# K^T V of a linear attention by 64x64 quadrants of TensorE, one head per quadrant

## The chip, the cores and the metric

The kernel runs on one core of a Trainium2 chip. The metric is the time of one execution in microseconds of the device. A profile is taken of one execution; its span, from the first to the last instruction, is about 2 us shorter than the time. The effect in this case is only about half a per cent, so traces are compared stage by stage, and the times come from several rounds (a round runs the compared kernels one after the other). TensorE's matmul side is PE in the profile and its weight loads are PEld; DVE is VectorE, ACT ScalarE, POOL GpSimd, SP the engine that issues most DMAs.

## The reference, cut to what matters

```python
# q, k, v: 8 batches, 8 heads, 576 positions, 64 values, float32
q_s = softmax(q, over the 64 values)
k_s = softmax(k, over the 576 positions)
kv  = einsum('bhsd,bhse->bhde', k_s, v)        # 64 x 64 per head: "K^T V"
x   = einsum('bhsd,bhde->bhse', q_s, kv)       # "X"; reordered to 4608 x 512
out = (silu(x @ w_gate) * (x @ w_val)) @ w_out # 512 -> 1536 -> 512
```

Nearly all arithmetic is in the last line. K^T V is small, but it runs on the same TensorE.

## The kernel before

A batch is handled in two groups G of four heads. A group's four heads are two row halves (g: partitions 0 to 63 and 64 to 127) times two column halves (h); `ek` holds exp(k), `vb` the values in bfloat16. Nine slices t of 64 positions are summed up in PSUM. A matmul takes the weights `lhsT` (here exp(k) of two heads, 64 rows x 128 columns) and streams `rhs` (the values of the same two heads and a column of ones, 129 values) past them. So it makes a 128 x 129 product, of which two 64 x 64 blocks are wanted and the last column is the softmax's sum:

```python
vbs = [const.tile([128, T, 130], BF16, ...) for i in range(2)]      # column 128 is ones

def kv_mm(b, G, kv, c):
    for t in range(T):                        # T = 9
        for g in range(2):
            r = slice(64 * g, 64 * g + 64)
            nc.tensor.matmul(
                out=kv[g][:, c:c + 129], lhsT=ek_of(b, G, g, t), rhs=vbs[G][r, t, 0:129],
                start=(t == 0), stop=(t == T - 1),
            )

def scale_both(b):                            # divide by the sum, on DVE
    ...
    nc.vector.reciprocal(out=kvr, in_=kv[:, :, 128])
    nc.vector.tensor_mul(kn[:, g], kv[:, :, 0:128], kvr.to_broadcast([128, NG, 128]))
```

X uses the wanted blocks as weights and the transposed q (`qt`) as stream; it already runs in 64x64 quadrants. In batches 2 to 7 `qt` comes from a transposing DMA, in batches 0 and 1 from TensorE. The order of TensorE's work:

```python
# batch 1 (after the first gate/value chunk), one group at a time
kv_one(1, 0); scale_one(1, 0, ...); norm_mul(1, 1)   # norm_mul: DVE makes qs
p = o_mm(2); x_one(1, 0); o_out(2, p)
turn_pe(1, 1, 0); turn_pe(1, 1, 1); ...              # transposes of qs on TensorE
kv_one(1, 1); scale_one(1, 1, ...)
p = o_mm(3); ... x_one(1, 1); o_out(3, p)

# batches 2 to 7: both groups together, within a chunk of 12 matmul units
for m in range(MT):
    ...                                              # exp, norm, turn_dma(b, G): qt by DMA
    if att and m == 8:
        kv_both(b); scale_both(b)
        if b + 1 < B: load_batch(b + 1)
    m_unit(c0, n, m)                                 # 8 matmuls of 448 or 512 values
    if att and m == 9:
        x_both(b)
```

The softmax here doesn't subtract the row's maximum and nothing guards it: scores larger than these inputs give would overflow.

## Time and profile before

| | before |
|---|---|
| time, median | 317.4 us |
| span in the profile | 316.2 us |
| PE busy | 306.3 us, 97% |
| granted TensorE clock | full (mean 1.000) |
| K^T V in the chain that ended last | about 3% |

From the page of the kernel before: its heading, the busy time of each engine (us, share of the span, instructions), and the start of the chain that ended last, that is of the work followed back from the last instruction.

```profile
span 316.2 us, 4851 instructions
PE 306.3 (97%) x1865; PEld 152.5 (48%) x1894; DVE 163.3 (52%) x277; ACT 147.1 (47%) x216; POOL 28.1 (9%) x35
PE 88%; DMA 4%; DVE 3%; ACT 2%; issue 1%; POOL 1%; SPq 0%; DVEq 0%
```

The third line is not a list of busy engines but of who was being waited for. That PE has 88% of it says more than its 97% busy time: the kernel ends when TensorE's stream of instructions ends.

The timeline of the kernel before around K^T V of batches 2 and 3 (start us, length us, engine, line, operation, output<-inputs, shape, count; in brackets the idle time before and what ended it):

```profile
66.13 1.22 PE L191 MATMUL kv<-vb,ek 64*128 64x129 bf16 x36
67.28 0.93 PE L298 MATMUL g_ps<-xt,wg 128*128 128x448 bf16 x4
70.42 0.69 PE L267 MATMUL xp<-qt,kn 64*64 64x512 bf16 x16
98.34 1.22 PE L191 MATMUL kv<-vb,ek 64*128 64x129 bf16 x36
99.50 0.82 PE L298 MATMUL g_ps<-xt,wg 128*128 128x512 bf16 x3
```

(A few records are missing: "x3" where there are four.)

### The profile page before, as it was taken

Reading aid. Unit: us, or ns where it says so; the run is one execution under the profiler, and the core shown is the slowest. Engines: PE = TensorE matmul, PEld = TensorE weight load, DVE = VectorE, ACT = ScalarE, POOL = GpSimd, SP = SyncE. Lnnn points to the kernel's source line nnn. Section 1 sums busy time; section 2 is a strip of 40 time slices with the busy share of each in tenths; the row PEclk is TensorE's granted clock in tenths of the full one; section 3 lists DMA queues with packets and bytes.
Section 4 is the critical chain, followed back from the end, with each engine's and each line's share of the span. In section 5 each row is a group of like instructions: output and inputs, shape, how many; then the busy total and the mean of one; then the engine's idle time right before and its main releaser. Section 6 shows DMA issues by size and latency. Waiting matters only on the chain.

```text
span 316.2 us, 4851 instructions
## 1 busy us (share of the span) xinstructions
PE 306.3 (97%) x1865; PEld 152.5 (48%) x1894; DVE 163.3 (52%) x277; ACT 147.1 (47%) x216; POOL 28.1 (9%) x35
## 2 busy tenths in 40 slices
PE   6999999999999999999999999999999999999994
PEld 2577744554444444544454444544444444444443
DVE  3734476685763567455835492639354333423421
ACT  4753397634663465447354637355743113312300
POOL 2930021101100020002000200020000000000000
PEclk9999999999999999999999999999999999999999
DMA  7999999269246906490629353944310202020124
GB/s 279 170 203 207 291 395 392 73 152 370 49 94 162 350 18 131 112 387 18 141 67 313 136 109 67 317 167 103 66 40 0 66 2 66 0 68 4 30 68 102
DMA packets 39304, 45.75 MB, mean 145 GB/s; under 512 B 16368, under 2 KB 23024, under 8 KB 39280
## 3 DMA queue, kind: packets, MB, share of 16 engines
q1 hardware_dynamic: 32480, 39.99, 42.0%
q0 software_dynamic: 6640, 5.31, 10.9%
q8 instruction: 15, 0.25, 0.3%
q10 hardware_dynamic: 160, 0.13, 0.2%
q14 instruction: 9, 0.07, 0.1%
HBM read 37.75 MB, written 9.44 MB: 149 GB/s over the span
## 4 chain that ended last, share of the span: by engine, by line
PE 88%; DMA 4%; DVE 3%; ACT 2%; issue 1%; POOL 1%; SPq 0%; DVEq 0%
PE g_ps L298 29%; PE u_ps L298 29%; PE o_ps L322 25%; PE kv L191 3%; DMA wv<-in_moe_w_val_dram 2%; DMA k<-in_k_dram 2%; DVE rs L138 1%; PE xp L267 1%; DVE qs L152 1%; PE o_ps L342 1%; ACT L124 1%; ACT eq L124 1%; POOL v L360 0%; PE tp L166 0%; POOL v L357 0%
## 5 line engine op out<-in xcount | busy, mean ns | idle before, releaser
L305 ACT ACTIVATE sg<-g_ps 128x512 bf16<-128x512 f32 (+2 forms) x120 | 65.2, 554 | 138.9 <-PE g_ps L298 119.4
L306 DVE TENSOR_TENSOR hr<-sg,u_ps 128x512 bf16<-128x512 bf16 (+2 forms) x120 | 74.5, 629 | 87.7 <-PE u_ps L298 80.3
L298 PE MATMUL g_ps<-xt,wg 128*128 128x512 bf16 (+2 forms) x469 | 110.0, 357 | 1.0 <-ACT xt L111 0.2
L298 PE MATMUL u_ps<-xt,wv 128*128 128x512 bf16 (+2 forms) x468 | 109.7, 357 | 1.0 <-DMA wv<-in_moe_w_val_dram 0.4
L322 PE MATMUL o_ps<-wo,hr 128*128 128x512 bf16 x414 | 93.0, 379 | 0.4 <-issue 0.2
L298 PEld LDWEIGHTS <-wv 128*128 128x128 bf16 x480 | 46.8, 98 | 47.2 <-DMA wv<-in_moe_w_val_dram 0.9
L298 PEld LDWEIGHTS <-wg 128*128 128x128 bf16 x480 | 45.8, 98 | 45.3 <-issue 0.9
L322 PEld LDWEIGHTS <-hr 128*128 128x128 bf16 x420 | 41.0, 98 | 49.1
L113 DVE COPY o_sb<-o_ps 128x512 f32<-128x512 f32 x33 | 22.4, 680 | 39.2 <-PE o_ps L322 37.3
L127 POOL CAST vb<-v 128x1152 bf16<-128x1152 f32 x14 | 16.1, 1148 | 173.5 <-DMA v<-in_v_dram 138.0
L138 DVE TENSOR_REDUCE rs<-eq 128x18 f32<-128x1152 bf16 (+2 forms) x18 | 21.7, 1214 | 12.8 <-ACT eq L124 12.8
L152 DVE TENSOR_TENSOR qs<-eq,rr 128x1152 bf16<-128x1152 bf16 (+2 forms) x18 | 22.0, 1232 | 0.1
L124 ACT ACTIVATE eq<-q 128x1152 bf16<-128x1152 f32 (+2 forms) x18 | 18.2, 1053 | 3.4 <-DMA q<-in_q_dram 3.4
L124 ACT ACTIVATE ek<-k 128x1152 bf16<-128x1152 f32 x16 | 18.0, 1159 | 0.7 <-DMA k<-in_k_dram 0.6
L305 ACT ACT_TABLE_LOAD x12 | 15.4, 1283 | 0.2
L124 ACT ACT_TABLE_LOAD x11 | 14.1, 1283 | 0.2
L387 PE MATMUL idle<-zero 128*128 128x512 bf16 x20 | 7.8, 555 | 2.7 <-DVE rs L138 1.5
L191 PE MATMUL kv<-vb,ek 64*128 64x129 bf16 x252 | 8.7, 217 | 0.0
L191 PEld LDWEIGHTS <-ek 64*128 64x128 bf16 x252 | 7.3, 94 | 2.7 <-ACT sg L305 2.1
L275 ACT CAST xt<-xp 128x512 bf16<-128x512 f32 x12 | 6.4, 589 | 3.6 <-PE xp L267 3.6
L276 DVE CAST xt<-xp 128x512 bf16<-128x512 f32 x12 | 7.7, 681 | 0.0
L113 DVE CAST xt<-xp 128x128 bf16<-128x128 f32 (+2 forms) x14 | 4.9, 374 | 2.8 <-PE xp L220 2.8
(45 smaller groups left out, 66.3 us busy)
## 6 DMA issues: line engine op xcount, KB each, us to landing
q<-in_q_dram SPq DMA_DIRECT2D x16, 576.0 KB, 5.3
k<-in_k_dram SPq DMA_DIRECT2D x16, 576.0 KB, 7.3
out_dram<-o_sb SPq DMA_DIRECT2D x70, 128.0 KB, 2.3
v<-in_v_dram SPq DMA_DIRECT2D x14, 576.0 KB, 9.0
wo<-in_moe_w_out_dram POOLq DMA_DIRECT2D x4, 384.0 KB, 16.4
wg<-in_moe_w_gate_dram POOLq DMA_DIRECT2D x2, 384.0 KB, 9.8
wv<-in_moe_w_val_dram POOLq DMA_DIRECT2D x2, 384.0 KB, 10.8
wg<-in_moe_w_gate_dram POOLq DMA_DIRECT2D x1, 512.0 KB, 13.8
```

The costliest lines, as they stand in the source:

```text
L113: eng.tensor_copy(out=out, in_=in_)
L124: nc.scalar.activation(out=e[:, t0:t1], in_=src[:, t0:t1], func=AF.Exp)
L127: nc.gpsimd.tensor_copy(out=vbs[G][:, :, 0:128].rearrange("p t (h d) -> p t h d", d=64), in_=raw["v", b, G].rearrange("p h (t d) -> p t h ...
L138: i = nc.vector.reduce_sum(out=rs[:, 2 * t0:2 * t1], in_=eq2[:, 2 * t0:2 * t1, :], axis=mybir.AxisListType.X)
L152: eng.tensor_mul(qs[:, t0:t1, :].rearrange("p t (h d) -> p (t h) d", d=64), eq2[:, 2 * t0:2 * t1, :], s["rr"][:, 2 * t0:2 * t1].to_broadca ...
L191: nc.tensor.matmul(out=kv[g][:, c:c + 129], lhsT=ek_of(b, G, g, t), rhs=vbs[G][r, t, 0:129], start=(t == 0), stop=(t == T - 1),)
L276: nc.vector.tensor_copy(out=xt[:, 2 * G + 1, c0:c0 + 512], in_=main[G][1])
L298: nc.tensor.matmul(out=gu[a][i][:, 0:w_], lhsT=(wg, wv)[a][:, kk, ms], rhs=xt[:, kk, c:c + w_], start=(kk == 0), stop=(kk == KT - 1),)
L305: nc.scalar.activation(out=sg[:, 0:w_], in_=g_ps[:, 0:w_], func=AF.Silu)
L306: nc.vector.tensor_mul(hr[:, m, r:r + w_], sg[:, 0:w_], u_ps[:, 0:w_])
L322: nc.tensor.matmul(out=o_ps, lhsT=hr[:, m, r0:r0 + 128], rhs=wo[:, m, :], start=(m == 0), stop=(m == MT - 1),)
L387: i = nc.tensor.matmul(out=idle, lhsT=zero[:, 0:128], rhs=zero, start=True, stop=True)
```

## The change: intent and diff

Half of the 128 x 129 product belongs to no head, as the two heads of a row half are crossed. The change gives each of the four heads its own quadrant, with 64 columns of weights and 65 streamed values, so that each matmul streams half as many values, and four heads are meant to run at once, as they do in X: in the trace before, the four quadrants of X start 3 to 4 ns apart (batch 3). The four matmuls of one slice, one in each quadrant, are called a four below; a pair is the two matmuls of a slice in the old form. It needs twice as many matmuls and weight loads, and a column of ones behind each head's values. Batch 0 takes its sums from elsewhere and streams 64 values.

```diff
-    vbs = [const.tile([128, T, 130], BF16, name=f"vb{i}", tag=f"vb{i}") for i in range(2)]
+    vbs = [const.tile([128, T, 2, 65], BF16, name=f"vb{i}", tag=f"vb{i}") for i in range(2)]
...
     def kv_mm(b, G, kv, c):
+        ek = st[b, G]["ek"]
         for t in range(T):
             for g in range(2):
-                r = slice(64 * g, 64 * g + 64)
-                nc.tensor.matmul(
-                    out=kv[g][:, c:c + 129], lhsT=ek_of(b, G, g, t), rhs=vbs[G][r, t, 0:129],
-                    start=(t == 0), stop=(t == T - 1),
-                )
+                for h in range(2):
+                    nc.tensor.matmul(
+                        out=kv[g][HALF[h], c:c + 65], lhsT=ek[HALF[g], t, h, :],
+                        rhs=vbs[G][HALF[g], t, h, :],
+                        start=(t == 0), stop=(t == T - 1),
+                    )
...  # scale_both; scale_one and scale_first alike
-            nc.vector.reciprocal(out=kvr, in_=kv[:, :, 128])
-            nc.vector.tensor_mul(kn[:, g], kv[:, :, 0:128], kvr.to_broadcast([128, NG, 128]))
+            nc.vector.reciprocal(out=kvr, in_=kv[:, :, 64])
+            nc.vector.tensor_mul(kn[:, g], kv[:, :, 0:64], kvr.to_broadcast([128, NG, 64]))
...  # x_mm, x_both: lhsT=kn[r, g, G, :] instead of kn[r, g, G, r]
...  # kv_first (batch 0): the same quadrants, 64 values instead of 128
```

More of the change, by code (lines that the diff above doesn't have):

```diff
@@ L127, in cast_v @@
         nc.gpsimd.tensor_copy(
-            out=vbs[G][:, :, 0:128].rearrange("p t (h d) -> p t h d", d=64),
+            out=vbs[G][:, :, :, 0:64],
             in_=raw["v", b, G].rearrange("p h (t d) -> p t h d", d=64),
@@ L182, in turn_dma @@
         nc.sync.dma_start_transpose(out=qt, in_=s["qs"].rearrange("p t c -> p (t c)"))
-    def ek_of(b, G, g, t):
-        return st[b, G]["ek"][64 * g:64 * g + 64, t, :, :].rearrange("p h d -> p (h d)")
+    HALF = (slice(0, 64), slice(64, 128))
     def kv_mm(b, G, kv, c):
+        ek = st[b, G]["ek"]
         for t in range(T):
             for g in range(2):
-                r = slice(64 * g, 64 * g + 64)
-                nc.tensor.matmul(
-                    out=kv[g][:, c:c + 129], lhsT=ek_of(b, G, g, t), rhs=vbs[G][r, t, 0:129],
-                    start=(t == 0), stop=(t == T - 1),
-                )
+                for h in range(2):
[4 more added lines that the diff above has]
+                    )
     def kv_one(b, G):
@@ L202, in scale_one @@
         s = st[b, G]
-        kn = s["kn"] = at.tile([128, 2, 128], BF16, tag="kn1", name="kn1")
+        kn = s["kn"] = at.tile([128, 2, 64], BF16, tag="kn1", name="kn1")
         for g in range(2):
@@ L206, in scale_one @@
             kvr = at.tile([128, 1], FP32, tag=f"kvr{g}", name="kvr")
-            nc.vector.reciprocal(out=kvr, in_=kv[:, 128:129])
+            nc.vector.reciprocal(out=kvr, in_=kv[:, 64:65])
             if engs[g] is nc.scalar:
-                nc.scalar.mul(kn[:, g, :], kv[:, 0:128], kvr)
+                nc.scalar.mul(kn[:, g, :], kv[:, 0:64], kvr)
             else:
-                nc.vector.tensor_scalar_mul(kn[:, g, :], kv[:, 0:128], kvr)
+                nc.vector.tensor_scalar_mul(kn[:, g, :], kv[:, 0:64], kvr)
     def x_mm(b, G, i):
@@ L221, in x_mm @@
                     out=xp[h][64 * g:64 * g + 64, 0:64 * (t1 - t0)],
-                    lhsT=s["kn"][r, g, r],
+                    lhsT=s["kn"][r, g, :],
                     rhs=s["qt"][r, t0:t1, 64 * g:64 * g + 64],
@@ L246, in scale_both @@
     def scale_both(b):
-        kn = st["kn", b] = at.tile([128, 2, NG, 128], BF16, tag="kn2", name="kn2")
+        kn = st["kn", b] = at.tile([128, 2, NG, 64], BF16, tag="kn2", name="kn2")
         for g in range(2):
@@ L268, in x_both @@
                             out=o[64 * g:64 * g + 64, c:c + n],
-                            lhsT=kn[r, g, G, r],
+                            lhsT=kn[r, g, G, :],
                             rhs=qt[G][r, t0:t1, 64 * g:64 * g + 64],
@@ L369 @@
         for vb in vbs:
-            nc.vector.memset(vb[:, :, 128:129], 1.0)
+            nc.vector.memset(vb[:, :, :, 64:65], 1.0)
         exp_of("q", 0, 0, BANKS)
@@ L408, in kv_first @@
                 for g in range(2):
-                    r = slice(64 * g, 64 * g + 64)
-                    nc.tensor.matmul(
-                        out=s["kv"][g][:, 0:128].rearrange("p (h d) -> p h d", d=64),
-                        lhsT=ek_of(0, G, g, t), rhs=v16[G][r, :, 64 * t:64 * t + 64],
-                        start=(t == 0), stop=(t == T - 1),
-                    )
+                    for h in range(2):
+                        nc.tensor.matmul(
+                            out=s["kv"][g][HALF[h], 0:64], lhsT=s["ek"][HALF[g], t, h, :],
+                            rhs=v16[G][HALF[g], h, 64 * t:64 * t + 64],
+                            start=(t == 0), stop=(t == T - 1),
+                        )
         def scale_first(G, eng1):
             s = st[0, G]
-            kn = s["kn"] = at.tile([128, 2, 128], BF16, tag="kn1", name="kn1")
-            nc.scalar.mul(kn[:, 0, :], s["kv"][0][:, 0:128], s["kvr"][:, 0:1])
+            kn = s["kn"] = at.tile([128, 2, 64], BF16, tag="kn1", name="kn1")
+            nc.scalar.mul(kn[:, 0, :], s["kv"][0][:, 0:64], s["kvr"][:, 0:1])
             if eng1 is nc.scalar:
-                nc.scalar.mul(kn[:, 1, :], s["kv"][1][:, 0:128], s["kvr"][:, 1:2])
+                nc.scalar.mul(kn[:, 1, :], s["kv"][1][:, 0:64], s["kvr"][:, 1:2])
             else:
-                nc.vector.tensor_scalar_mul(kn[:, 1, :], s["kv"][1][:, 0:128], s["kvr"][:, 1:2])
+                nc.vector.tensor_scalar_mul(kn[:, 1, :], s["kv"][1][:, 0:64], s["kvr"][:, 1:2])
         spin(8)
```

## The prediction

> **What bounds the kernel.** TensorE: the page's busy table has PE at 97% of 316.2 us at full granted clock, and the chain of waits lies 88% on PE. PE's stream counts almost one for one; K^T V is a small part, 2.6% of the chain.
>
> **The stage today.** In the timeline a batch's K^T V is 36 matmuls of 64 rows x 128 columns with 129 values, six times, plus four single groups (batches 0 and 1) of 18. Single records show the two row halves starting 3 ns apart and pairs 57 ns apart: 18 pairs, 1.03 us, plus 0.1 us before and after, where the tile shape changes.
>
> **What the change does.** Per batch 72 weight loads and 72 matmuls of 65 values instead of 36 and 36 (order listing: 576 more PE instructions in all). The scaling on DVE (424 ns) halves, but lies in the shadow of a full matmul unit.
>
> **The array's own limit.** [...] 64x64 loads read [64,1,1] and take 103 to 107 ns, 64x128 loads [32,1,4] and 92 to 95. But quadrant matmuls of the X stage with 64 values show no bar: fours start 28 ns apart, the second four's weights issued only 26 ns before. So the array could do 18 fours in about 0.5 us: 0.5 us gained a batch, 4 us in all.
>
> **The instruction stream's limit.** I expect this to bind. PE's only semaphore instructions in mid-kernel tell where its sequencer is. In the steady 512-value stretch the one ahead of K^T V runs 33 instructions before its turn (94.43 us, against 98.39). [...] this trace shows about 33. The next, 104 instructions after the stage's first, runs at 99.565, though room for it had come by 99.40; the same in all five batches. So I estimate that the sequencer was behind, delivering 104 - 33 = 71 instructions in 1.18 us: 16.6 ns each. Today's stage takes one each 14.3 ns and lives off the 33 in the queue; fours at 28 ns would take one each 3.5 ns. After some 40 instructions the queue is empty and the rest come at 16.6: (144 - 33) x 16.6 = 1.84 us instead of 1.03, +0.8 us x 6. Single groups: (72 - 33) x 16.6 = 0.65 against 0.52, +0.13 each. Sum +5 us, nearly all on the critical path.
>
> **Prediction.** If the sequencer limits, about 322.5 us; if the array does, 313.5. I give the first two chances in three. Predicted 321.5 us, 8 in 10 within 312.8 to 325.0. Chances: faster by over 2% 0.03, within 2% 0.79, slower 0.18.
>
> **What would show it.** Right: the stage spans about 1.9 us a batch in the timeline; the first few fours are about 28 ns apart, later ones about 130 ns; PE idles for "issue". Wrong: fours evenly 28 to 30 ns apart and a stage of 0.5 us; or fours evenly 55 ns apart (quadrant loads not hidden behind quadrant matmuls), and an unchanged time.
>
> **What would make it wrong.** The 16.6 ns rests on one inference; the late semaphore instruction may have another cause. [...] A gain over 2% needs 6 us; I see no source for it.

## More of the kernel before

A batch's K^T V holds PE for 1.15 us, from its own start to the start of the next matmul.

The single records of this stage show two row halves starting 3 to 4 ns apart, and pairs 59 ns apart on average (1.006 us from first to last start; single distances 55 to 68 ns).

In batch 1 nothing is waited for long. These are pieces of the chain that ended last, in order of time, in the kernel before:

```profile
43.53 1.37 DVE qs L152
44.95 0.68 PE tp L166 x9
45.62 0.63 PE kv L191 x18
46.41 2.54 PE o_ps L322 x11
48.95 0.37 PE xp L220 x8
49.32 0.61 PE tp L166 x9
```

Here the chain runs through PE itself from 44.95 us on: each piece starts where the one before it ends, but for 0.16 us of "issue" at 46.25 us.

## The result, and the profile after

The changed kernel takes 315.69 us in the median of 6 runs (315.24 to 315.98), the kernel before 317.41 (317.16 to 317.55). The ratio is 0.9946, 95% interval 0.9934 to 0.9959. (Ratios here are the mean time of one kernel's fast runs over that of the other's in the same rounds, so not quite the ratio of the medians.) So it is half a per cent faster, where I had predicted 321.5 us, slower.

The same lines of the page after:

```profile
span 313.8 us, 5456 instructions
PE 304.8 (97%) x2182; PEld 149.8 (48%) x2182; DVE 161.6 (51%) x277; ACT 147.1 (47%) x216; POOL 28.1 (9%) x35
PE 87%; DMA 8%; DVE 2%; POOL 1%; ACT 1%; issue 0%; SPq 0%; ACTq 0%
```

What stands out is DMA: 8% of the chain instead of 4%. Hold that for a moment. The timeline of the changed kernel at the same two places:

```profile
65.47 0.81 PE L191 MATMUL kv<-vb,ek 64*64 64x65 bf16 x72
69.33 0.41 PE L268 MATMUL xp<-qt,kn 64*64 64x512 bf16 x4
70.13 0.47 PE L268 MATMUL xp<-qt,kn 64*64 64x512 bf16 x12 [0.39 <-DMA qt<-qs]
97.84 0.89 PE L191 MATMUL kv<-vb,ek 64*64 64x65 bf16 x72
98.66 1.04 PE L299 MATMUL g_ps<-xt,wg 128*128 128x512 bf16 x4
```

The stage of batch 3 takes 0.82 us (97.84 to 98.66) instead of 1.16. It did not become 1.9 us, so the instruction supply did not bind as I had expected. But in batch 2 PE now stops in the middle of X, waiting for the transposed q. And the chain that ended last now has pieces that are not PE's:

```profile
34.85 8.32 DMA q<-in_q_dram
43.19 1.17 ACT eq L124
44.39 1.36 DVE rs L138
46.78 1.99 DVE qs L152
48.81 0.68 PE tp L166 x9
65.50 4.58 DMA qt<-qs
70.13 0.47 PE xp L268 x12
```

Read from the top: the load of batch 1's second q ends at 43.17 us; its exp, row sum and normalisation lead to the transposes at 48.81. So from 34.85 to 48.81 us the end of the kernel hung on a load and not on PE. Later the transposing DMA of batch 2 does the same.

Where the time went, from the starts of the last gate-times-value product (DVE) of each chunk, which both traces have complete:

| stretch | before | after | difference |
|---|---|---|---|
| start to end of chunk 0 (batch 0) | 40.08 | 39.48 | -0.60 |
| batch 1, to the first product of chunk 1 | 18.19 | 18.12 | -0.07 |
| chunk 1, with K^T V and X of batch 2 | 16.07 | 16.24 | +0.17 |
| chunks 2 to 6 (batches 3 to 7) | 165.32 | 163.54 | -1.78 |
| rest, to the end of the span | 76.55 | 76.38 | -0.17 |

A chunk of batches 3 to 7 took 33.06 or 33.07 us before and takes 32.64 to 32.73 after. Batches 1 and 2 gained next to nothing. The first line is an accident of one execution: in other traces of these kernels chunk 0 ends between 39.2 and 39.8 us, whichever form K^T V has.

So there were three questions. Why was the supply of instructions no limit? What sets the new pace? And why do batches 0 to 2 show no gain?

### The profile page after: what moved, and what is told of

The parts are those of the page before. It is cut to its first block, busy times and chain, and to the rows that moved or that the text cites. A ratio compares the mean times of both kernels' runs of the same rounds, so it can differ in the third digit from the quotient of the medians.

```text
span 313.8 us, 5456 instructions
## 1 busy us (share of the span) xinstructions
PE 304.8 (97%) x2182; PEld 149.8 (48%) x2182; DVE 161.6 (51%) x277; ACT 147.1 (47%) x216; POOL 28.1 (9%) x35
## 4 chain that ended last, share of the span: by engine, by line
PE 87%; DMA 8%; DVE 2%; POOL 1%; ACT 1%; issue 0%; SPq 0%; ACTq 0%
PE g_ps L299 29%; PE u_ps L299 28%; PE o_ps L323 26%; DMA q<-in_q_dram 3%; DMA wv<-in_moe_w_val_dram 2%; DMA k<-in_k_dram 2%; DMA qt<-qs 1%; PE kv L191 1%; PE xp L268 1%; PE o_ps L343 1%; DVE qs L152 1%; POOL v L361 0%; DVE rs L138 0%; ACT eq L124 0%; POOL v L358 0%
## 5 line engine op out<-in xcount | busy, mean ns | idle before, releaser
L299 PE MATMUL g_ps<-xt,wg 128*128 128x512 bf16 (+2 forms) x480 | 111.6, 358 | 0.2 <-ACT xt L111 0.2
L299 PE MATMUL u_ps<-xt,wv 128*128 128x512 bf16 (+2 forms) x480 | 111.2, 358 | 0.3 <-DMA wv<-in_moe_w_val_dram 0.3
L113 DVE COPY o_sb<-o_ps 128x512 f32<-128x512 f32 x33 | 22.4, 680 | 39.2 <-PE o_ps L323 39.2
L191 PEld LDWEIGHTS <-ek 64*64 64x64 bf16 x504 | 5.2, 106 | 2.7 <-ACT sg L306 2.1
L191 PE MATMUL kv<-vb,ek 64*64 64x65 bf16 x504 | 6.1, 195 | 0.0
```

The costliest lines, as they stand in the source:

```text
L113: eng.tensor_copy(out=out, in_=in_)
L191: nc.tensor.matmul(out=kv[g][HALF[h], c:c + 65], lhsT=ek[HALF[g], t, h, :], rhs=vbs[G][HALF[g], t, h, :], start=(t == 0), stop=(t == T - 1),)
L299: nc.tensor.matmul(out=gu[a][i][:, 0:w_], lhsT=(wg, wv)[a][:, kk, ms], rhs=xt[:, kk, c:c + w_], start=(kk == 0), stop=(kk == KT - 1),)
```

## The experiments

Two theories for the third question. **A:** the quadrants make TensorE's stage shorter everywhere, but in batches 0 and 1 a load that arrives at a fixed time takes the gain back, and in batch 2 the transposing DMA does, which an instruction fetch has delayed. **B:** these waits are accidents of one execution, and all stages' gains add up. For the pace: the streamed values, the supply of instructions, or something in the array such as the loading of weights.

### again: the changed kernel once more

No edit.

> The changed kernel once more, for a second trace and more rounds. Theory A (two gains are given back by fixed causes: in batch 2 an instruction fetch of 16 KB lies on the transposing DMA of qt, and in batch 1 the transposes wait for qs on DVE): the trace shows both waits again, 0.39 us for qt and 0.32 us for qs, and again a stage of 0.60 or 0.67 us a batch. Rival B (both waits were an accident of one execution): they are gone or elsewhere. Ratio to before 0.994 to 0.996 either way.

Measured: 315.68 us, ratio 0.9945 (0.9925 to 0.9965). The wait for qs is there (0.20 us), the wait for qt is not; X of batch 2 only took 0.84 us instead of 0.69. Chunk 1 took 15.81 us. So the wait for qt differs from one execution to the next: part of theory A was too rigid. The stages of batches 2 to 7 are the same to a few ns.

The records of single DMA packets suggest why. Two queues on the page are marked "instruction": q8, with packets of 16 KB, and q14. The change, which adds 576 instructions to PE's stream and none to the other engines', raises q8 from 15 packets to 17 and leaves q14 at 9; so I take q8's packets for fetches of PE's instructions. In the trace after, the one in batch 2 took 0.93 us (all of them 0.92 to 1.76). Where such a packet meets the transposing DMA, whose 256-byte packets take 0.018 us in the median, the longest of these takes 1.24 to 1.74 us (the third column; in the trace after 19 of them take over 1 us):

| trace | fetch in batch 2, us | its longest transpose packet, us | slowest qt landing, us | PE waits for qt |
|---|---|---|---|---|
| before | 62.14, ahead of the transposes | 0.14 | 3.3 | 0 |
| after | 67.43 | 1.42 | 4.6 | 0.39 |
| again | 66.78 | 1.24 | 4.2 | 0 |
| shift_fetch | 66.57 | 1.63 | 4.5 | 0.3 |
| narrow | 67.16 | 1.56 | 4.9 | 0.71 |
| x2_later (below) | 67.52 | 1.74 | 5.0 | 0, hidden |

With the additional instructions of the change the fetch lies on the transposes (67.43 us) and not ahead of them (62.14). This is a coincidence in time, but a regular one: in all eight traces in which a fetch lies on batch 2's transposes the slower qt lands after 4.2 to 5.0 us, and in all five others, with the fetch ahead of them or behind, after 3.2 to 3.3 us. The single late packets are not always there (x2_second, below: landing 4.7 us, longest packet 0.11 us), and the delay is not the same everywhere: in batch 4 of the changed kernel a fetch at 120.21 us cost its transposes only some 0.4 us. From the DMA queues on the two pages (queue, kind, packets, MB, share of the DMA engines' time), before:

```profile
q8 instruction: 15, 0.25, 0.3%
```

and after:

```profile
q8 instruction: 17, 0.28, 0.4%
```

Two more packets in all, and 0.1% more of the DMA engines' time: if the fetch is the cause, it is by what one of them happens to lie upon.

### shift_fetch: 40 more instructions ahead of everything

```diff
-            for _ in range(n):
-                i = nc.tensor.matmul(out=idle, lhsT=zero[:, 0:128], rhs=zero, ...)
+            for _ in range(2 * n):
+                i = nc.tensor.matmul(out=idle[:, 0:256], lhsT=zero[:, 0:128], rhs=zero[:, 0:256], ...)
```

> The changed kernel, with each of the 20 warm-up matmuls of 512 values split into two of 256: the same array time at the start, but 40 more TensorE instructions ahead of everything else, so that every instruction fetch comes some 20 matmuls (about 4 us) earlier. If the fetch delays the qt transpose of batch 2 (theory A), its landing takes 3.2 to 3.3 us again instead of 4.6, the wait of PE for qt in batch 2 is gone and the kernel gains 0.4 to 0.6 us on the changed one. If the wait comes from PE being earlier alone (rival), landing and wait stay and the time does too. A fetch may then fall on another transpose, where there is more slack.

Measured: 315.55 us, ratio 0.9931 (0.9915 to 0.9947), PE waits 0.3 us for qt. The fetch came only 0.9 us earlier and still lay on the transposes, most likely because the 40 instructions are passed within the burst of K^T V, 144 instructions in some 0.6 us, and not at the slow pace that I had reckoned with. So the experiment doesn't tell the causes apart. Nearest to the run that was meant comes both_only (below): batch 2 has the quadrants, the transposes start at nearly the same time (65.73 us, against 65.50), but the fetch comes at 61.61 us, ahead of them. There qt lands after 3.3 us and PE does not wait. A run with the fetch moved and nothing else was not made, so that the fetch causes the late landing rests on these traces; that PE waits for this landing is in the timeline.

### x2_later and x2_second: X of batch 2 one unit later

```diff
-                if att and m == 9:
+                if att and m == (10 if ci == 0 else 9):
                     x_both(b)
```

> The changed kernel, with the X stage of batch 2 alone one matmul unit later (after unit 10 instead of unit 9, 1.5 us later). Theory A: the wait for qt is hidden, 0.4 to 0.6 us less than the changed kernel (ratio to it about 0.9985). Rival: the time given back in batch 2 has another cause and nothing changes.

Measured: 314.88 us, ratio 0.9914 (0.9896 to 0.9931). In its trace the qt landing takes up to 5.0 us, the slowest of all, and PE does not wait for it: the wait is hidden. Chunk 1 takes 15.66 us, against 16.24 and 15.81 in two traces of the changed kernel. That is 0.15 to 0.6 us, less than the 0.8 us by which the times differ. In this trace batch 1's load also came early (its q landed at 42.73 us, against 43.17 and 43.07), so PE didn't wait for qs either; the rest may be such scatter. It was run again:

> x2_later again. If its 0.8 us over the changed kernel were real in full, 0.992 or less; if only the wait for qt is hidden, as the traces say (0.15 to 0.6 us in chunk 1), it beats the changed kernel by 0.15 to 0.6 us, ratio to before 0.9925 to 0.994; if the first result was scatter, equal to changed_third.

> The changed kernel a third time, on the same chip and in the same rounds as x2_second: ratio to before 0.9945. In its trace batch 2 waits for qt by 0 to 0.7 us, as the instruction fetch happens to fall on the transpose earlier or later (traces so far: 0.39 and 0).

In the same rounds on one chip: changed_third 315.60 us in the median of its five fast runs (315.39 to 315.76), x2_second 315.12 (314.56 to 315.50). So 0.5 us, as expected, and in the same direction as the first time. The ratios to before, 0.9921 (0.9886 to 0.9956) and 0.9905 (0.9869 to 0.994), are both lower than expected, with wide intervals, because the kernel before scattered up to 320.61 us in these rounds.

### both_moves and before_moves: a second wait, and the control

Besides x2_later's move, four of the twelve matmuls of output tile 3 come before the transposes that wait for qs:

```diff
         o_out(2, p)
+        p = o_mm(3, None, 0, 4)
         turn_pe(1, 1, 0)
...
-        p = o_mm(3)
+        p = o_mm(3, p, 4, MT)
```

> As x2_later, and also four of the twelve matmuls of output tile 3 moved ahead of the transposes of batch 1's second group, so that these need not wait for qs. Theory A: the 0.32 us wait is hidden too, together 0.7 to 0.9 us less than the changed kernel, ratio to before about 0.992. If the moved matmuls only move the wait to kn or xt, it equals x2_later.

Measured: 315.22 us, ratio 0.9925 (0.991 to 0.9939). Not better than x2_later: PE's wait for qs is gone from its waits, but a wait for xt has grown from 0.2 to 0.6 us, and batch 1's stretch takes 18.19 us as before. The wait was moved, not removed.

> The control: the kernel before, with the same two moves as both_moves (X of batch 2 one unit later, four matmuls of output tile 3 earlier). If the moves only uncover what the quadrants gained, the kernel before has nothing to uncover: 1.000 +- 0.001. If the moves are a gain of their own, it is faster by the 0.5 to 0.8 us by which x2_later beat the changed kernel. It is also a second trace of the old start, to tell whether the start was 0.4 us slower in the first by chance.

Measured: 317.64 us, ratio 0.9998 (0.9979 to 1.0016). The kernel before gains nothing from the same moves. So x2_later's move is worth something only once the quadrants have made PE early. The trace ends chunk 0 at 39.57 us with the old form, no later than the changed kernel (39.48, 39.71): the -0.60 us in the table above was chance.

### both_only and single_only: the change in two halves

In both_only batches 0 and 1 are in the old form, in single_only batches 2 to 7 are (cut to one of the places):

```diff
# both_only, kv_one
-        kv_mm(b, G, s["kv"], 0)
+        ...     out=s["kv"][g][:, 0:130], lhsT=(64 rows x 128 columns), rhs=vbs[G][HALF[g], t, :, :]
# single_only, kv_both
-            kv_mm(b, G, kv, 256 * G)
+            ...     out=kv[g][:, 256 * G:256 * G + 130], lhsT=(64 rows x 128 columns), rhs=vbs[G][HALF[g], t, :, :]
```

> Quadrants only in the six batches whose two groups are done together (2 to 7); batches 0 and 1 in the old form (64 rows x 128 columns; in batch 1 with 130 values). Theory A (batches 0 and 1 are held by the arrival of batch 1's loads, so that quadrants gain nothing there): as the changed kernel, ratio to before 0.994 to 0.995. Rival (each stage's gain adds up): 0.44 us or more is lost against the changed kernel, ratio 0.996.

> The complement: quadrants in batches 0 and 1 only, the other six in the old form with 130 values. Theory A: no gain, ratio 0.999 to 1.001. Rival: 0.44 us from batch 1 and as much from batch 0, ratio 0.997 to 0.998.

Measured: both_only 315.23 us, ratio 0.9933 (0.9912 to 0.9954); single_only 317.66 us, ratio 1.001 (0.9979 to 1.0042). So nearly all of the gain comes from the six double batches. Rival B in full, 0.9 us from batches 0 and 1, doesn't fit: five of the six runs of single_only are between 317.0 and 317.8 us, like the kernel before (the sixth, 320.54, alone brings the ratio from 0.9996 to 1.001). A gain of 0.2 us can't be seen in these times. Nor is both_only a clean proof that these batches give nothing: it had no wait for qt, so it is to be compared with the versions in which that wait is hidden (314.88, 315.12 and 315.22 us), and against these, measured in other rounds, it is 0 to 0.35 us slower. Why the gain is small can be read in the chain of single_only, again in order of time:

```profile
34.69 8.87 DMA q<-in_q_dram
43.58 1.17 ACT eq L124
44.77 1.36 DVE rs L138
47.16 1.82 DVE qs L152
49.03 0.68 PE tp L166 x9
```

In this execution TensorE had chunk 0 done early (at 39.19 us, against 40.08 in the trace of the kernel before), and PE then waited 0.8 us for the transposes' input: the exp of batch 1's second q could start at 43.58 us, when its load had landed, much as in the others (43.50 before, 43.19 after, 43.09 again). A shorter K^T V ahead of that only lengthens the wait.

But the second group's K^T V of batch 1 comes behind that wait, and there the traces show a small gain. From the second group's transposes to the first product of chunk 1 it takes 9.01 us in the three traces with the old form in batch 1 (before, both_only, twice_before), and 8.77 to 8.79 in the eight with quadrants and the same order (single_only 8.79). So theory A holds for batch 0 and the first group of batch 1; the second group keeps its 0.22 us. In both_only's trace the fetch of batch 2 came at 61.61 us, ahead of the transposes, and chunk 1 took 15.66 us, the same as in x2_later, without any wait for qt. Two pieces of its chain, K^T V and X of batch 2, both PE's:

```profile
65.75 0.74 PE kv L191 x72
69.62 0.62 PE xp L277 x16
```

### narrow: half the streamed values

```diff
-                        out=kv[g][HALF[h], c:c + 65], lhsT=ek[HALF[g], t, h, :],
-                        rhs=vbs[G][HALF[g], t, h, :],
+                        out=kv[g][HALF[h], c:c + (33 if t else 65)], lhsT=ek[HALF[g], t, h, :],
+                        rhs=vbs[G][HALF[g], t, h, 0:(33 if t else 65)],
```

> One look, wrong result on purpose: the changed kernel in which all but the first four of each group take 33 values instead of 65. Fours in the trace are 29 to 36 ns apart now, 31.7 on average. If the streamed values set that, they come 15 to 20 ns apart. If instruction supply (8 instructions at about 4.2 ns is 33 ns) or the loading of 64 columns of weights sets it, they stay near 32 ns and the stage stays at 0.6 us. My prediction's 16.6 ns an instruction would give 130.

Measured: a wrong result, as meant; one time, 315.47 us. Distances in ns of the starts of successive fours in one batch (single records; 18 fours, so 17 distances), batch 6 of each, the changed kernel first:

```
after   53 36 29 34 29 35 29 34 29 35 29 32 30 31 36 29 37
narrow  53 32 32 32 31 32 32 31 32 32 31 32 32 31 32 32 38
```

With 33 values the pace is the same as with 65, 32 ns. So the streamed values do not set it. Neither, as I read it, does the supply of instructions at that point: within the second to fourth fours of the changed kernel the weight loads and matmuls start 3 to 4 ns apart (late in the stage 8 to 9 ns), so they were at hand, and yet these fours are no closer than the later ones. What sets the 32 ns instead is not shown: no run tells the loading of 64 columns of weights from a fixed cost of each matmul in its quadrant.

### twice_after and twice_before: everything in the stage done twice

```diff
-        for t in range(T):
+        for i, t in enumerate(times * list(range(T))):          # times=2 in kv_both
...
-                        start=(t == 0), stop=(t == T - 1),
+                        start=(i == 0), stop=(i == times * T - 1),
```

> The changed kernel, with every matmul of K^T V of batches 2 to 7 done twice into the same accumulation (sums double, the quotient and the result stay). 288 instructions a batch at once[...]. If the array sets the pace (31.7 ns a four), the stage grows by 18 x 31.7 = 0.57 us a batch, 3.4 us in all against the changed kernel. If the sequencer does (about 4.2 ns an instruction, seen at the end of the stage), the second half runs at 33 ns a four and more, plus a stall of 65 ns each 128 instructions or so, 0.7 us a batch, 4.2 us. At my predicted 16.6 ns it would be 144 x 16.6 = 2.4 us a batch, 14 us.

> The same for the kernel before: 18 pairs more a batch at 57 ns, 1.03 us a batch, 6.2 us in all, with no stalls, if its pace of 14.3 ns an instruction is the array's. At the predicted 16.6 ns of supply the second half would run at 66 ns a pair, 7.2 us in all. The difference between the two doubled kernels should be that between the plain ones plus 2 to 2.8 us.

Measured: twice_after 318.77 us, ratio 1.0044 (1.0029 to 1.0059), 3.1 us over the changed kernel; twice_before 323.81, ratio 1.0202 (1.0185 to 1.0219), 6.4 us over the kernel before. Both results are correct. The 3.1 us is less than either of the figures expected (3.4 and 4.2): chunks 2 to 6 together grew by 3.17 us, while chunk 1 took 16.43 us, against 16.24, as in batch 2 the longer stage fell into the wait for qt. The two doubled kernels so differ by 3.3 us more than the plain ones, and not by 2 to 2.8. This is the clearest refutation of the prediction: at 16.6 ns an instruction twice_after would have cost 14 us more than the changed kernel. The timeline of twice_after, batch 2, has 144 matmuls, and their weight loads with them, in 1.5 us:

```profile
65.15 1.50 PE L191 MATMUL kv<-vb,ek 64*64 64x65 bf16 x144
```

That is 288 instructions in 1.3 us (the last matmul's own 0.2 us taken off, 195 ns in the trace after), 4.6 ns each with its one stall. In the traces the later fours of a doubled stage are 31 to 36 ns apart, 33.5 on average away from the stalls, that is 8 instructions at 4.2 ns; late in the stage the weight loads start 8 or 9 ns apart, 8.3 on average, with a matmul to each (in the plain changed kernel too, from about the 13th four on), where those of a four early in the stage start 3 to 4 ns apart. This even spacing, in place of fours in quick succession, looks like a supply limit of about 4.2 ns an instruction; no run tests it by itself. The quadrants at 4.0 ns an instruction (32 ns a four) lie right at it, and the old form at 14.8 (59 ns a pair) far from it: twice_before goes on at 59 ns a pair on average (the 2.28 us below, less 0.22 us of the last matmul's own, over 35 distances), 34.11 us a chunk instead of 33.06. Its stage in batch 2:

```profile
65.98 2.28 PE L191 MATMUL kv<-vb,ek 64*128 64x129 bf16 x72
```

The stalls are a second, small effect. In batches 3, 4, 5 and 7 of the changed kernel about the 128th instruction of the stage comes 67 to 78 ns late (71 to 80 ns after the matmul before it; a stage of 0.67 to 0.68 us instead of 0.59 from first to last start); in batches 2 and 6 none does. In twice_after it is the 209th in batch 2, and the 126th to 129th in the others. It doesn't coincide with a fetch packet in the records. Its cause stays open; it costs about 0.3 us in the whole kernel.

## Why the prediction was wrong

The semaphore instruction from which the prediction took its 16.6 ns runs five times (ns of one; first and last start in us; PEldq is PE's sequencer ahead of a weight load), in the kernel before:

```profile
L267 PEldq EVENT_SEMAPHORE  x5: 51/51/51, 99.5 to 231.8; - x5
```

and in twice_before:

```profile
L267 PEldq EVENT_SEMAPHORE  x5: 51/51/51, 101.5 to 237.9; - x5
```

- **"I expect this to bind": the supply of instructions at 16.6 ns each. This step failed.** It rested on one semaphore instruction that ran late, at a place where I held that the queue had room. The doubled kernels speak against that reading. In the kernel before it runs 0.165 to 0.168 us after the last K^T V matmul starts, and 7 to 9 ns after the second weight load of the next unit starts. In twice_before, with twice the instructions ahead, it runs just as long after: 0.166 to 0.168 us, and 7 to 9 ns. A sequencer that lagged by some ns for each instruction would lag more there. So most likely it was held until TensorE took its next instructions: where the tile shape changes, the next unit's first weight load starts 0.143 to 0.145 us after the start of the last K^T V matmul (0.12 to 0.14 us in the changed kernel). As I now read it, I took a full queue for a slow sequencer. What stops the semaphore instruction where it runs (29 instructions ahead here, 33 in the steady stretch, both counted in the trace after) is not known. The even spacing late in the doubled stage, which I take for the supply, is about 4.2 ns an instruction, a quarter of the 16.6.
- **"So the array could do 18 fours in about 0.5 us: 0.5 us gained a batch." Right in kind, too large.** A batch's stage, from first start to last, went from 1.006 to 0.593 us where no stall fell into it and to 0.67 to 0.68 where one did, as fours come 32 ns apart and not 28, and the second 53 after the first. The gain in batches 3 to 7 is 0.33 to 0.42 us each, 1.78 us in all. The 28 ns had been read from two fours of X, of which the first had its weights loaded some 215 ns ahead, in the shadow of matmuls of 512 values.
- **"Nearly all on the critical path", and the 4 us of the other branch. Wrong for batches 0 to 2.** Batch 0 and the first group of batch 1 are held by the load of batch 1's q (single_only: 1.001; PE waits 0.8 us for qs); only the second group gains, 0.22 us. In batch 2 PE came early enough to meet the transposing DMA, which landed 1.3 us late in the trace after, most likely because of an instruction fetch; 0.15 to 0.6 us of the chunk's time went there. I had seen the slack neither of the load nor of the transposes, having looked only for waits that were already there.
- **The ledger.** Six double batches 0.42 + 1.78 = 2.2 us; less 0.15 to 0.6 in batch 2: 1.6 to 2.05; with the 0.22 of batch 1, 1.8 to 2.3. Measured: 317.41 - 315.69 = 1.7 us, and 1.8 in again; a difference of 0.1 to 0.5 us is within the scatter of the start (chunk 0 alone ends between 39.2 and 40.1 us). both_only, whose fetch fell elsewhere: 2.1 us.
- **Right:** PE is the bound in batches 3 to 7, where what its stage saves is saved in the time; the scaling and the cast are hidden (in the trace after PE's waits name neither in batches 2 to 7); no gain over 2%.

The best version seen is the changed kernel with X of batch 2 one unit later: 314.9 and 315.1 us, 0.5 to 0.8 us below the changed kernel in the same rounds.

## What to carry to other kernels

Where a change shortens the bounding engine's work, ask of each stage not only what it waits for now but how soon it would begin to wait: an early stage fed by loads, or a result of a DMA that is just in time, can give the gain back, as the load of batch 1's q (PE waited 0.8 us for qs in single_only) and qt of batch 2 (0.39 us in the trace after) did here, and the chain then shows the load or DMA instead of the engine. An instruction that runs late need not show a slow sequencer: here it ran 0.165 to 0.168 us after the last matmul of the stage, and as long after with the stage doubled. Look at what was issued just ahead of it, and double the stream to tell the two apart. Quadrants paid here even though they double the instructions, but a four of them took the same 32 ns with 33 values as with 65.
